# Output-projection blocks of the last layer as rows, and the final conversion to bf16 on ScalarE alone

## The chip, the cores and the metric

The kernel runs on one core of a Trainium2 chip. The metric is the device time of one execution in microseconds, the lower the better. The granted clock is the share of its full clock that TensorE had in a stretch by the profile.

## The reference

Four attention layers for one token, which use the weights and caches A, B, A, B in turn. Each layer normalizes x (640 values), makes 32 queries of 192, attends over a cache of 8192 keys and values per head, projects with wo and adds the result to x.

```python
def _A_ref(x, k_cache, v_cache, wq, wo):
    q = (x @ wq).reshape(B, Sq, Hq, Dh) ...                    # 640 -> 32 heads x 192
    scores = jnp.einsum("bhqd,bhkd->bhqk", q, k) * (Dh ** -0.5) # 8192 keys per head
    p = _softmax(scores, axis=-1)
    o = jnp.einsum("bhqk,bhkd->bhqd", p, v)
    return o.reshape(B, Sq, Hq * Dh) @ wo                       # 6144 -> 640

x = A_x
x = x + _A_ref(_layernorm(x, axis=-1), A_k_cache, A_v_cache, A_wq, A_wo)
x = x + _B_ref(_layernorm(x, axis=-1), B_k_cache, B_v_cache, B_wq, B_wo)
x = x + _A_ref(...)                                             # layer 2, A again
x = x + _B_ref(...)                                             # layer 3, B again
```

## The kernel before

The caches are streamed through eight slots of on-chip memory. VectorE multiplies k by the query, and TensorE sums the products through an identity matrix, makes the softmax's weighted sum of v, and projects. The projection is done in blocks of five pairs of heads (`wo` blocks 0, 1 and 2; the third is cut in two parts, the later one called `wob`) and a last pair (`wol`). PSUM is the memory into which the matmuls write; a bank is one piece of it, and a quadrant, in this text, is 32 neighbouring partitions (rows). The parts that matter:

```python
def op(self, fn, *events, ..., bank=()):
    for d in bank:                                  # one record per PSUM bank:
        self.wait(*[ev for q, ev in d.items() if q is not self])   # wait for every other engine's last use
    ...

def project(n, w, o, ev_o):                         # y as columns: 128 x 5 values
    PE.wait(ev_o, need(n), last["YB"])
    for i in range(k):                              # k = 15 in a whole block
        for c in range(DC):                         # DC = 5
            e = PE.op(... t.matmul(YB[:, c:c + 1], lhsT=t3[:, i, c:D:DC], rhs=o[:, i:i + 1], ...))
    freed[n] = e                                    # the slot of these weights is free
    return e

def project_row(n, w, o, ev_o):                     # y as two rows of 320, on partitions 0 and 32
    for i in range(k):
        for h in range(2):
            e = PE.op(... t.matmul(YR[32 * h:32 * h + 1, :], lhsT=o[:, i:i + 1],
                                   rhs=t3[:, i, h * HD:(h + 1) * HD], ...))
    return e

def to_row(ev):                                     # x + y so far, from columns to the rows
    e = DV.op(... z = x_true + YB[:, 0:DC], ev, ev_true, bank=YBu)
    ...                                             # z split into three bf16 parts on VectorE
    PE.op(... zero the rows ...)                    # 1 matmul
    for i in range(3):                              # 3 x 5 x 2 = 30 matmuls with the identity
        ...

elif n[0] == "wo":
    last["oT"] = (project_row if l == 3 and n[2] == 2 else project)(...)
    if l == 3 and n[2] == 1:
        to_row(last["oT"])
...                                                 # after the last layer:
a, m = slot[...][0:33, 0:HD], 192
return a, (DV.op(lambda v: v.tensor_copy(a[:, 0:m], YR[:, 0:m]), ev_y, last["oT"], bank=YBu),
           AC.op(lambda c: c.activation(a[:, m:], YR[:, m:], ACT.Copy), ev_y, last["oT"], bank=YBu))
```

Shortly before the end the kernel issues filler matmuls (`busy(16)` and `busy(6)`), whose result nobody reads.

## Time and profile before

| | before |
|---|---|
| time, 3 runs known at the prediction | 1985.24 us median, 1982.80 to 1987.34 |
| span of the profiled execution | 1980.6 us |
| bytes read, rate over the span | 848.36 MB, 428 GB/s |
| busiest compute engine | TensorE, 65% |
| last load lands | 1973.88 us |
| from there to the end of the span | 6.7 us |

### The profile page before, as it was taken

The page shows a single profiled execution, that of the slowest core. Times are in us where ns is not written, and L with a number is a line of the kernel's source. Part 1 is how long each engine was busy: PE and PEld are TensorE (multiplying, and loading weights), DVE is VectorE, ACT ScalarE, POOL GpSimd, SP SyncE. Part 2 cuts the span into 40 slices and gives each one's busy share as a digit, 9 for nine tenths or more (in the row PEclk, how much of TensorE's full clock was granted, in tenths as well). Part 3 has the DMA queues.
Part 4 walks back from the last instruction along what each step waited for, and adds up shares of the span by engine and source line. Part 5 has one row for each costly group of instructions (what it writes and reads, how often), then busy time and mean ns, then how long its engine had stood idle before and what let it go on. Part 6 is the DMA issues. An engine that isn't in the chain of part 4 may idle for free.

```text
span 1980.6 us, 13926 instructions
## 1 busy us (share of the span) xinstructions
PE 1282.8 (65%) x8335; PEld 148.6 (8%) x3249; DVE 1201.2 (61%) x1377; ACT 139.6 (7%) x462; POOL 4.5 (0%) x23
## 2 busy tenths in 40 slices
PE   3567476566466666666785675666676766667658
PEld 0001001000100100100020010010002001001001
DVE  3566466467166656566745565665764765665756
ACT  0000000000000000000010000000000100000000
POOL 0000000000000000000000000000000000000000
PEclk9787777778687777777887777877886877777778
DMA  9999999999999999999999999999999999999998
GB/s 413 437 432 430 430 430 432 436 430 428 435 431 431 430 435 433 428 433 433 427 408 432 427 430 431 430 430 431 431 431 428 436 429 434 432 432 431 431 434 364
DMA packets 26786, 849.25 MB, mean 429 GB/s; under 512 B 3042, under 2 KB 3044, under 8 KB 3812
## 3 DMA queue, kind: packets, MB, share of 16 engines
q1 hardware_dynamic: 26580, 848.38, 99.6%
q8 instruction: 45, 0.74, 0.2%
q14 instruction: 17, 0.14, 0.0%
q10 hardware_dynamic: 144, 0.00, 0.0%
HBM read 848.36 MB, written 0.00 MB: 428 GB/s over the span
## 4 chain that ended last, share of the span: by engine, by line
DMA 67%; PE 17%; DVE 15%; ACT 1%; issue 0%; SPq 0%
DMA pool<-in_B_k_cache_dram 27%; DMA pool<-in_A_v_cache_dram 22%; DMA pool<-in_A_k_cache_dram 13%; DVE pool L595 13%; PE S L58 7%; DMA pool<-in_B_v_cache_dram 6%; PE OY L58 5%; PE OY L674 3%; DVE acc L693 1%; ACT p_sb L632 1%; DVE s_sb L617 1%; PE OY L535 1%; PE S L608 0%; DVE m_bf L619 0%; PE QM L622 0%
## 5 line engine op out<-in xcount | busy, mean ns | idle before, releaser
L595 DVE TENSOR_TENSOR pool<-pool,q_sb 128x3072 bf16<-128x3072 bf16 x512 | 860.8, 1751 | 231.9 <-DMA pool<-in_B_k_cache_dram 133.3
L58 PE MATMUL S<-pool,ident 128*128 128x512 bf16 x2944 | 788.6, 425 | 20.4 <-DVE pool L595 18.8
L704 PE MATMUL TB<-acc,small 128*1 128x192 f32 x240 | 82.7, 495 | 212.0 <-DVE acc L693 212.0
L58 PE MATMUL OY<-pool,p_sb 128*16 128x512 bf16 x1920 | 198.8, 490 | 0.0
L608 PE MATMUL S<-pool,ident 128*128 128x512 bf16 x128 | 62.4, 488 | 207.7 <-DVE pool L595 207.6
L692 DVE TENSOR_SCALAR acc<-OY,small 128x192 f32<-128x192 f32 x64 | 26.7, 418 | 277.9 <-PE OY L58 248.0
L674 PE MATMUL OY<-pool,p_sb 128*16 128x512 bf16 (+1 forms) x1216 | 145.9, 488 | 64.3 <-DMA pool<-in_A_v_cache_dram 59.7
L693 DVE SCALAR_TENSOR_TENSOR acc<-OY,small,acc 128x192 f32<-128x192 f32 x424 | 177.0, 418 | 14.9
L617 DVE TENSOR_REDUCE s_sb<-S 128x64 f32<-128x512 f32 x128 | 87.8, 686 | 68.0 <-PE S L58 68.0
L524 ACT ACTIVATE q_sb<-QM 128x192 bf16<-128x192 f32 x60 | 19.8, 330 | 952.4 <-PE QM L518 952.4
L715 ACT ACTIVATE rows<-TB,small 1x192 bf16<-1x192 f32 x120 | 43.1, 405 | 587.7 <-PE TB L704 587.7
L688 DVE RECIPROCAL small<-TB 1x2 f32<-1x2 f32 x64 | 11.2, 175 | 94.7 <-PE TB L647 75.3
L632 ACT ACTIVATE p_sb<-s_sb,small 64x128 bf16<-64x128 f32 x128 | 55.7, 435 | 160.9 <-DVE small L626 160.1
L608 PEld LDWEIGHTS S<-pool,ident 128*128 128x128 bf16 x128 | 12.9, 101 | 682.9 <-DVE pool L595 619.9
L647 PE MATMUL TB<-small,ones 128*1 128x2 f32 x120 | 11.4, 165 | 74.1 <-ACT p_sb L632 74.1
L674 PEld LDWEIGHTS OY<-pool,p_sb 128*16 128x16 bf16 (+1 forms) x1216 | 38.9, 105 | 207.4 <-issue 133.1
L622 PE MATMUL QM<-ident,m_bf 128*64 128x64 bf16 x128 | 14.1, 217 | 54.4 <-DVE m_bf L619 53.8
L704 PEld LDWEIGHTS TB<-acc,small 128*1 128x1 f32 x240 | 19.8, 102 | 311.2 <-DVE acc L693 284.0
L535 PE MATMUL OY<-oT,pool 128*128 128x1 bf16 x825 | 34.9, 178 | 2.5 <-ACT oT L580 2.5
L626 DVE TENSOR_REDUCE small<-QM 128x1 f32<-128x64 f32 x64 | 14.3, 224 | 35.2 <-PE QM L622 35.2
L535 PEld LDWEIGHTS OY<-oT,pool 128*128 128x128 bf16 x825 | 33.9, 131 | 4.5 <-ACT oT L580 3.2
L518 PEld LDWEIGHTS QM<-rows,one_b 1*64 1x64 bf16 x120 | 6.2, 100 | 347.1 <-issue 341.2
(75 smaller groups left out, 205.0 us busy)
## 6 DMA issues: line engine op xcount, KB each, us to landing
pool<-in_B_k_cache_dram SPq DMA_DIRECT2D x28, 6144.0 KB, 38.1
pool<-in_B_v_cache_dram SPq DMA_DIRECT2D x28, 6144.0 KB, 33.5
pool<-in_A_v_cache_dram SPq DMA_DIRECT2D x27, 6144.0 KB, 27.6
pool<-in_A_k_cache_dram SPq DMA_DIRECT2D x34, 3072.0 KB, 19.9
pool<-in_A_k_cache_dram SPq DMA_DIRECT2D x14, 6144.0 KB, 36.5
pool<-in_A_v_cache_dram SPq DMA_DIRECT2D x10, 3072.0 KB, 14.3
pool<-in_B_k_cache_dram SPq DMA_DIRECT2D x8, 3072.0 KB, 22.4
pool<-in_A_wo_dram SPq DMA_DIRECT2D x6, 2400.0 KB, 22.1
```

The lines of the kernel that those rows point to most:

```text
L58: return t.add_instruction(mybir.InstMatmult(name=t.bass.get_next_instruction_name(), engine=mybir.EngineType.PE, ins=[t.lower_ap(rhs), t. ...
L524: lambda a: a.activation(q_sb[i][:], QM[:, 0:DH], ACT.Copy), e, last["q"][i], bank=QMu)
L535: e = PE.op(lambda t, i=i, c=c, f=y_first[0], fin=n[0] == "wol" and i == k - 1: t.matmul(YB[:, c:c + 1], lhsT=t3[:, i, c:D:DC], rhs=o[:, i ...
L595: e = DV.op(lambda v, d0=d0: v.tensor_tensor(k3[:, :, d0:d0 + QD], kin[:, :, d0:d0 + QD], q_sb[qi][:, d0:d0 + QD].unsqueeze(1).broadcast_t ...
L608: t.matmul(S[:, :], lhsT=ident[:], rhs=k3[:, :, d0:d0 + R], start=True, stop=fin) if d0 == 0 else
L617: lambda v, u=u: v.tensor_reduce(s[:, u * JU:(u + 1) * JU], SP_[u][:].rearrange("p (j r) -> p j r", r=R), AX.X, ALU.add), ev_S[p, u], last ...
L632: ev_p[p] = AC.op(lambda a, h=h, r=r: a.activation(p_sb[par][r, :, h], s[r, :], ACT.Exp, bias=negm[par][r, 0:1], accum_out=l_col[par][r, h ...
L674: t.matmul(o, lhsT=x, rhs=y, start=f, stop=fin) if c == 0 else
L692: v.tensor_scalar(acc[:], O[:, 0:DH], pick[:, 0:1], None, ALU.mult) if i == 0 else
L693: v.scalar_tensor_tensor(out=acc[:], in0=O[:, i * DH:(i + 1) * DH], scalar=pick[:, i:i + 1], in1=acc[:], op0=ALU.mult, op1=ALU.add)), e if ...
L704: e = PE.op(lambda t, h=h: t.matmul(TB[96:97, C_O + h * DH:C_O + (h + 1) * DH], lhsT=half[:, h:h + 1], rhs=acc[:], start=True, stop=True), ...
L715: last["TO"] = last["row_written"] = AC.op(lambda a, h=h: a.activation(orow[:, o0 + h * DH:o0 + (h + 1) * DH], TB[96:97, C_O + h * DH:C_O ...
```

## The change

The intent is to have one form of the projection in layer 3. Its blocks 0 and 1 become rows too, so that 30 matmuls replace 75 in each. The residual then no longer waits for block 1: it is turned into the row ahead of block 0, and VectorE's wait for the product falls away. The final conversion is one ScalarE copy in place of two half copies on two engines.

```diff
-            def to_row(ev):
-                e = DV.op(lambda v: v.tensor_tensor(z[:], x_true[:], YB[:, 0:DC], ALU.add), ev, ev_true, bank=YBu)
+            def to_row():
+                e = DV.op(lambda v: v.tensor_copy(z[:], x_true[:]), ev_true)
                 ...
-                PE.wait(e, ev_const)
+                PE.wait(e, ev_const, last["YB"])
@@ project_row
+                if n[0] == "wo" and n[2] < 2:
+                    freed[n] = e
@@ layer
-                    last["oT"] = (project_row if l == 3 and n[2] == 2 else project)(...)
-                    if l == 3 and n[2] == 1:
-                        to_row(last["oT"])
+                    if l == 3 and n[2] == 0:
+                        to_row()
+                    last["oT"] = (project_row if l == 3 else project)(...)
@@ end
-                a, m = slot[place[("wo", 3, 2)]][0:33, 0:HD], 192
-                return a, (DV.op(... tensor_copy(a[:, 0:m], YR[:, 0:m]) ...), AC.op(... a[:, m:], YR[:, m:] ...))
+                a = slot[place[("wo", 3, 2)]][0:33, 0:HD]
+                return a, AC.op(lambda c: c.activation(a, YR, ACT.Copy), ev_y, last["oT"], bank=YBu)
```

(The output transfer then waits for one event and not for two. Cuts are marked with dots.)

More of the change, by code (lines that the diff above doesn't have):

```diff
@@ L541, in project @@
                 return e
-            def to_row(ev):
-                src = z
-                e = DV.op(lambda v: v.tensor_tensor(z[:], x_true[:], YB[:, 0:DC], ALU.add), ev, ev_true, bank=YBu)
+            def to_row():
+                e = DV.op(lambda v: v.tensor_copy(z[:], x_true[:]), ev_true)
                 for i in range(3):
@@ L740, in layer @@
                     k = NW - NB[l] if n[2] == 2 else NW
-                    last["oT"] = (project_row if l == 3 and n[2] == 2 else project)(n, slot[place[n]][:, 0:k * D], oT[:, 0:k], last["oTw"])
-                    if l == 3 and n[2] == 1:
-                        to_row(last["oT"])
+                    if l == 3 and n[2] == 0:
+                        to_row()
+                    last["oT"] = (project_row if l == 3 else project)(n, slot[place[n]][:, 0:k * D], oT[:, 0:k], last["oTw"])
                 elif n[0] == "wob":
@@ L757, in layer @@
             if l + 1 == NL:
-                a, m = slot[place[("wo", 3, 2)]][0:33, 0:HD], 192
-                return a, (DV.op(lambda v: v.tensor_copy(a[:, 0:m], YR[:, 0:m]), ev_y, last["oT"], bank=YBu),
-                           AC.op(lambda c: c.activation(a[:, m:], YR[:, m:], ACT.Copy), ev_y, last["oT"], bank=YBu))
+                a = slot[place[("wo", 3, 2)]][0:33, 0:HD]
+                return a, AC.op(lambda c: c.activation(a, YR, ACT.Copy), ev_y, last["oT"], bank=YBu)
             ev_z = DV.op(lambda v: v.tensor_tensor(z[:], xc[:], YB[:, 0:DC], ALU.add), ev_y, ev_xc, bank=YBu)
@@ L767, in build @@
             ev_z, ev_true = layer(l, ev_z, ev_true)
-        e = SP.op(lambda s: s.dma_start(out[0, 0].rearrange("(h n) -> h n", h=2), ev_z[0:33:32, :]), *ev_true, sem=semOUT, inc=16)
+        e = SP.op(lambda s: s.dma_start(out[0, 0].rearrange("(h n) -> h n", h=2), ev_z[0:33:32, :]), ev_true, sem=semOUT, inc=16)
         SP.wait(e)
```

## The prediction

> **What bounds the kernel now.** I read the page from the top: the shares, the forty slices, then the chain of waits at its end, then the order of time around the places that the diff touches. The slices come first, because they say which resource never rests.
>
> ```profile
> PE 1282.8 (65%) x8335; PEld 148.6 (8%) x3249; DVE 1201.2 (61%) x1377; ACT 139.6 (7%) x462; POOL 4.5 (0%) x23
> DMA  9999999999999999999999999999999999999998
> HBM read 848.36 MB, written 0.00 MB: 428 GB/s over the span
> pool<-in_B_v_cache_dram SPq DMA_DIRECT2D x28, 6144.0 KB, 33.5
> ```
>
> No compute engine is busy for more than 65%, and the DMA row reads 9 in every slice but the last. 848.36 MB in 1980.6 us is 428 GB/s, so the span is the time of the transfers plus what lies before the first and after the last of them. The fourth line gives the depth of the queue: one load of 6144 KB (6.29 MB) takes 6.29/428 = 14.7 us at that rate, but the median from issue to landing is 33.5 us. So a load is issued with more than one other load ahead of it, and a delay of its issue by a few us leaves the stream unbroken. Only two kinds of change move the time: fewer bytes or a gap in that stream, and work after the last load has landed. The diff changes no byte, and a comparison of the instruction orders shows the DMA-issuing engine's own list of instructions the same in both kernels.
>
> The work after the last landing is read from the chain of waits, in order of time:
>
> ```profile
> 1936.56 37.33 DMA pool<-in_B_v_cache_dram
> ...
> 1975.73 0.89 PE TB L700 x12
> 1976.62 1.20 PE OY L568 x16
> 1977.82 0.02 issue
> 1977.84 0.36 DVE pool L759
> 1978.20 0.02 issue
> 1978.22 0.27 ACT pool L760
> ```
>
> The last load lands at 1973.88. From there to the end of the span are 6.7 us, all serial. The reader should see the last three pieces of work: the 16 row matmuls of layer 3's last block, then VectorE's copy of 192 columns to bf16, and then ScalarE's copy of the other 128. They are written as two halves of one job on two engines, but they run one after the other. The waits say so too: ScalarE sat idle "1.30 <-DVE pool L759" before its copy, though the matmuls had been over for 0.4 us by then. The cause is in the code: each operation on the row's PSUM bank first waits for the last operation of every other engine on that bank, reads included. The split therefore gains nothing.
>
> The third view is the order of time around layer 3's second wo block, where the diff has its largest piece:
>
> ```profile
> 1802.01 3.16 PE L535 MATMUL OY<-oT,pool 128*128 128x1 bf16 x75 [0.28 <-ACT oT L580]
> 1805.20 0.33 SPq L376 DMA_DIRECT2D pool<-in_B_v_cache_dram  x1
> 1805.20 0.16 DVE L546 TENSOR_TENSOR small<-small,OY 128x5 f32<-128x5 f32 x1 [6.84 <-PE OY L535]
> ...
> 1806.44 0.45 PE L552 MATMUL OY<-ident,zero 128*33 128x320 bf16 x1 [1.27 <-DVE part L548]
> 1806.82 1.48 PEld L557 LDWEIGHTS OY<-ident,part 128*1 128x1 bf16 x30 [0.28 <-issue]
> 1806.82 1.76 PE L557 MATMUL OY<-ident,part 128*1 128x64 bf16 x30
> 1809.15 13.44 DVE L595 TENSOR_TENSOR pool<-pool,q_sb 128x3072 bf16<-128x3072 bf16 x8 [2.77 <-DMA pool<-in_B_k_cache_dram]
> ```
>
> 75 column matmuls (3.16 us) end the block and release its weights' slot, so the next v load is issued. Then VectorE adds and splits the residual (six operations, until 1806.38) and TensorE turns it into a row (until 1808.58). After that VectorE still waits 2.77 us, and for a DMA: the next k tile lands at 1809.15, whatever this block does.
>
> **What the Trainium skill says.** "DMA: Bandwidth & Descriptors", section Bandwidth, measures 425 GB/s for 16 MB with one core streaming, and puts the ceiling at 435. The trace agrees: 428 over the whole span and 430 to 437 in most slices. There is no room left in the stream.
>
> "PSUM — Partial Sum Buffer", section on PSUM bank collisions, says that two engines must not touch the same bank and quadrant at once, two readers included. Both copies read the same bank in the same two quadrants, so the wait between them is needed and not an oversight; the trace shows it kept.
>
> "ScalarE: Activation LUTs", section What ACT_TABLE_LOAD costs, gives 186 ns + 0.833 ns per column for an ACTIVATE with immediate scale and bias. The trace is a little below: 185 ns for 15 columns (198 by the formula), 270 for 128 (293) and 330 for 192 (346). For 320 columns the formula gives 453 ns; less the 16 to 23 ns by which it is high at 192 and 128 columns, I take 0.43 us.
>
> "TensorE: Matmul & The Clock Gate", Part 1, says that the clock falls to half after an idle stretch of about 3.4 us. The stretches agree: the granted clock is 0.50 through both wo blocks, at 1651.8 to 1655.1 and at 1802.0 to 1805.2, and 1.00 in the tail, where the kernel runs filler matmuls first. This matters for the price of a row matmul.
>
> **The change part by part.**
>
> Part one, blocks 0 and 1 as rows. Each loses 75 column matmuls at 3.16/75 = 42 ns and gains 30 row matmuls of 320 columns. In the tail 16 of those took 1.20 us with 0.30 us for a single one, so (1.20 - 0.30)/15 = 60 ns from one to the next, at clock 1.00. At 0.50 I take twice that, 120 ns: 29 x 0.12 + 0.45 = 3.9 us (estimate). So a block becomes about 0.8 us longer, not shorter, if the clock stays down; with a full clock it would be 29 x 0.06 + 0.30 = 2.0 us, 1.1 us shorter. The instruction count alone, 30 for 75, misleads here.
>
> Part two, the residual moved. At block 0 its six VectorE operations (1805.20 to 1806.38, so 1.2 us; the first becomes a copy of as many elements) need no product of the block and can run as soon as VectorE has finished the fifth pair's accumulation, at 1648.2. VectorE then idles 9.85 us until a k tile lands at 1658.06, so they are hidden. TensorE's 31 matmuls (0.38 us to the next start and 1.76 us, some 2.1 us) now stand between the columns and the block's own products. The block's end, and with it the issue of the v load that waits for its slot, moves from 1655.06 to about 1655.1 + 2.1 - 0.2 (the wait for oT, now covered) + 0.8 = 1657.8, 2.7 us later. The queue then still holds the k load that was issued at 1644.62 and lands only at 1687.1. So nothing empties. TensorE's next matmuls begin at 1659.88, which is 2 us after.
>
> At block 1 the v load is issued some 0.8 us later than at 1805.20 (or 1.1 us earlier, at a full clock), and TensorE is free at about 1806 in place of 1808.6. VectorE's 6.84 us wait there is gone. Its next product still starts when the k tile lands at 1809.15, so this is worth 0 us.
>
> Part three, the final row. On the path, from 1977.84 to 1978.49, are 0.36 + 0.02 + 0.27 = 0.65 us. One ScalarE copy of 320 columns replaces it with 0.43 us and the same start: after a PE result the two engines begin within 0.02 us of each other in the trace (1976.62 to 1976.65 for ScalarE, 1977.82 to 1977.84 for VectorE). Saved: 0.22 us. The output transfer waits for one semaphore in place of two, which I count as 0.
>
> Sum: 0 + 0 - 0.22 = -0.2 us, or 0.01%. From the median of 1985.24 that gives 1985.0.
>
> **The rivals.** First, the later v load at block 0 opens a gap in the stream. For it speaks only that the issue does move, by an estimated 2.7 us. Against it stands the backlog: the loads issued at 1637.67 and 1644.62 are both still unfinished at 1655.06, near 2 x 14.7 = 29 us of work. Even if all of it came through, the time would be 1987.7, still within 2%.
>
> Second, the freed time counts in full: the removed VectorE wait (6.84 us), the shorter TensorE work after block 1 (2.6 us) and the tail (0.2 us) would give 1975.6, 0.5% faster. For it speaks that VectorE is busy 61% and holds 15% of the chain. Against it: the wait after it is for a DMA (the 2.77 us at 1809.15), and time freed on an engine that waits for data returns as a longer wait. I think it unlikely.
>
> Third, ScalarE could be slower from PSUM over 33 partitions than I reckon. If its copy took 0.65 us, the tail would be as before: 1985.2.
>
> **Range and chances.** All that the change can do is smaller than the noise: the three runs before lie at 1982.80, 1985.24 and 1987.34, 4.5 us apart. The range follows from that spread and not from the rivals: 1985.0 with 4.5 us to each side, 1980.5 to 1989.5. A change of 2% would be 40 us. Neither rival comes near it, so within 2% gets 0.99, and each side 0.005.
>
> **What would show it right or wrong.** The tail: ScalarE's copy of 33x320 starts some 0.03 us after the last row matmul and lasts 0.41 to 0.46 us, with no VectorE operation near it; from the last landing to the span's end pass 6.5 us in place of 6.7. The blocks: 30 row matmuls in 3.4 to 4.2 us at a granted clock of 0.50; if they take about 2 us, my scaling with the clock fails. At block 0 TensorE's 31 residual matmuls come ahead, and the v load is issued 2 to 3 us later after the wait for the matmuls' end; its landing does not move against its neighbours. At block 1 VectorE waits once, for the k tile. The rate stays at 428 GB/s over the span. I am wrong if the DMA row shows a slice under 9 around 1640 to 1700, if the chain passes through the row matmuls of blocks 0 or 1, or if the time moves by more than the runs scatter.

## The result, and the profile after

| | before | after |
|---|---|---|
| time, 6 runs each | 1983.33 us median, 1982.80 to 1987.34 | 1983.21 us median, 1982.22 to 1984.94 |
| ratio | | 0.9996, 95% interval 0.9983 to 1.0009 |
| span of the profiled execution | 1980.6 us | 1980.6 us |
| last load lands | 1973.88 | 1974.19 |
| last landing to end of span | 6.7 us | 6.4 us |

A ratio is the mean time of one kernel's runs over that of the other's of the same rounds, so it is not quite the ratio of the medians quoted. Executions over 1.5% slower than the fastest of the same kernel are left out of the means.

The time is the same within what the timer can tell. The changed kernel is right. Its stream of transfers, from the page's forty slices (first the busy tenths of the DMA engines, then the bytes they moved):

```profile
DMA  9999999999999999999999999999999999999998
GB/s 413 435 435 429 430 430 433 436 428 429 436 430 431 430 435 433 427 433 432 426 412 431 426 429 432 431 428 432 431 430 428 435 431 435 431 432 432 431 432 367
HBM read 848.36 MB, written 0.00 MB: 428 GB/s over the span
```

Nothing has changed there. Blocks 0 and 1 of layer 3 fall into slices 34 and 37 of 40, and no slice from there on dips but the last, as before. Next the order of time around block 0 (start, length, engine, line, operation; in brackets the idle time before it and what ended it), first before, then after:

```profile
1644.62 0.33 SPq L376 DMA_DIRECT2D pool<-in_B_k_cache_dram  x1
...
1651.88 3.16 PE L535 MATMUL OY<-oT,pool 128*128 128x1 bf16 x75 [0.28 <-ACT oT L580]
1655.06 0.33 SPq L376 DMA_DIRECT2D pool<-in_B_v_cache_dram  x1
1658.06 3.43 DVE L595 TENSOR_TENSOR pool<-pool,q_sb 128x3072 bf16<-128x3072 bf16 x2 [9.85 <-DMA pool<-in_B_k_cache_dram]
```

```profile
1645.01 0.33 SPq L376 DMA_DIRECT2D pool<-in_B_k_cache_dram  x1
...
1648.52 0.16 DVE L545 COPY small<-small 128x5 f32<-128x5 f32 x1
...
1651.92 0.45 PE L551 MATMUL OY<-ident,zero 128*33 128x320 bf16 x1
1652.30 1.76 PE L556 MATMUL OY<-ident,part 128*1 128x64 bf16 x30
1653.81 4.07 PE L567 MATMUL OY<-pool,oT 128*1 128x320 bf16 x30
1657.92 0.33 SPq L376 DMA_DIRECT2D pool<-in_B_v_cache_dram  x1
1658.28 5.09 DVE L596 TENSOR_TENSOR pool<-pool,q_sb 128x3072 bf16<-128x3072 bf16 x3 [8.58 <-DMA pool<-in_B_k_cache_dram]
```

The residual's VectorE work (from 1648.52) is done while VectorE would wait for the k tile. TensorE's part of it and the rows follow each other, and the v load goes out when the rows end. Counted from the k load ahead of it, it is issued 12.9 us later; before it was 1655.06 - 1644.62 = 10.4 us. Block 1 after, in the same view:

```profile
1802.26 4.16 PE L567 MATMUL OY<-pool,oT 128*1 128x320 bf16 x30 [0.28 <-ACT oT L581]
1806.46 0.33 SPq L376 DMA_DIRECT2D pool<-in_B_v_cache_dram  x1
1810.01 3.43 DVE L596 TENSOR_TENSOR pool<-pool,q_sb 128x3072 bf16<-128x3072 bf16 x2 [11.41 <-DMA pool<-in_B_k_cache_dram]
```

VectorE's wait of 6.84 us for the block's products is gone. In its place stands one wait of 11.41 us for the k tile: the freed time has come back as a longer wait for data. (The tile lands 0.86 us later than before. Already the k load of block 0, which no part of the change precedes, was issued 0.39 us later in this trace, and the last landing is later by 0.31 us.) The waits of the DMA-issuing engine tell the same of the v loads behind both blocks (who waited for whom: us in total, times, longest), first before, then after:

```profile
SPq L376 <- PE OY L535: 20.2, 2, 10.1
```

```profile
SPq L376 <- PE OY L567: 23.7, 2, 12.6
```

The queue's issuer waited 3.5 us longer in all for the two blocks, and the stream did not notice. Last, the end of the chain of waits after the change:

```profile
1936.94 37.25 DMA pool<-in_B_v_cache_dram
...
1976.93 1.20 PE OY L567 x16
1978.13 0.02 issue
1978.15 0.43 ACT pool L760
```

One copy of 0.43 us stands where VectorE's 0.36, a gap of 0.02 and ScalarE's 0.27 stood. Around blocks 0 and 1 the chain runs along the k loads (one of 42.31 us from 1645.01 on) and not through the row matmuls, as the prediction had it.

### The profile page after: what moved, and what is told of

Its sections match the earlier page's. It is cut to its first block, busy times and chain, and to the rows that moved or that the text cites. A ratio compares the mean times of both kernels' runs of the same rounds, so it can differ in the third digit from the quotient of the medians.

```text
span 1980.6 us, 13743 instructions
## 1 busy us (share of the span) xinstructions
PE 1288.7 (65%) x8245; PEld 146.4 (7%) x3159; DVE 1201.3 (61%) x1376; ACT 139.9 (7%) x462; POOL 4.5 (0%) x23
## 3 DMA queue, kind: packets, MB, share of 16 engines
HBM read 848.36 MB, written 0.00 MB: 428 GB/s over the span
## 4 chain that ended last, share of the span: by engine, by line
DMA 67%; PE 19%; DVE 12%; ACT 1%; issue 0%; SPq 0%
DMA pool<-in_B_k_cache_dram 27%; DMA pool<-in_A_v_cache_dram 22%; DMA pool<-in_A_k_cache_dram 13%; DVE pool L596 10%; PE S L58 10%; DMA pool<-in_B_v_cache_dram 6%; PE OY L58 5%; PE OY L675 3%; DVE acc L694 1%; ACT p_sb L633 1%; DVE s_sb L618 1%; PE S L609 1%; PE OY L535 0%; DVE m_bf L620 0%; PE QM L623 0%
## 5 line engine op out<-in xcount | busy, mean ns | idle before, releaser
L693 DVE TENSOR_SCALAR acc<-OY,small 128x192 f32<-128x192 f32 x64 | 26.7, 418 | 281.1 <-PE OY L58 251.6
L689 DVE RECIPROCAL small<-TB 1x2 f32<-1x2 f32 x64 | 11.2, 175 | 94.9 <-PE TB L648 75.2
L609 PEld LDWEIGHTS S<-pool,ident 128*128 128x128 bf16 x128 | 12.9, 101 | 683.1 <-DVE pool L596 589.1
L535 PE MATMUL OY<-oT,pool 128*128 128x1 bf16 x675 | 28.6, 178 | 1.9 <-ACT oT L581 1.9
L535 PEld LDWEIGHTS OY<-oT,pool 128*128 128x128 bf16 x675 | 27.8, 131 | 3.8 <-ACT oT L581 2.5
```

Of the source, the lines that this page charges most:

```text
L535: e = PE.op(lambda t, i=i, c=c, f=y_first[0], fin=n[0] == "wol" and i == k - 1: t.matmul(YB[:, c:c + 1], lhsT=t3[:, i, c:D:DC], rhs=o[:, i ...
L609: t.matmul(S[:, :], lhsT=ident[:], rhs=k3[:, :, d0:d0 + R], start=True, stop=fin) if d0 == 0 else
L693: v.tensor_scalar(acc[:], O[:, 0:DH], pick[:, 0:1], None, ALU.mult) if i == 0 else
```

## The experiments

My theory: the stream of loads sets the time, a backlog of nearly 30 us in its queue hides whatever the wo blocks do, and the only part of the change on the path is the final copy, some 0.2 us. The rivals: a later issue of a load counts in full; TensorE's work does not matter at all; the rows themselves gain time that the later issue eats up.

**How late may a load be issued?** Two kernels take the changed kernel and make block 0 later, by filler matmuls of which the result is not read.

```diff
                     if l == 3 and n[2] == 0:
+                        busy(88)      # late40: busy(180)
                         to_row()
```

> The changed kernel with 88 filler matmuls (about 20 us of TensorE: some 8 at half clock, the rest at full) ahead of the residual's turn to a row at layer 3's first wo block, so that the v load that waits for the slot of this block's weights is issued some 18 us later. Backlog theory: the k load ahead of it in the queue lands only near 1687, so the stream does not empty; ratio to before 0.999 to 1.001, no gap in the transfers. Rival (a later issue counts in full): +18 us, ratio 1.009. By the way: the 30 row matmuls then run at a granted clock of 1.00 and take 2.0 to 2.2 us in place of 4.07.

Measured: right output, 1982.41 us median against 1983.21 for the kernel before, ratio 0.9998 (0.9983 to 1.0013). From the order of time:

```profile
1651.99 20.19 PE L58 MATMUL S<-ident 128*128 128x512 bf16 x87
...
1673.16 2.23 PE L567 MATMUL OY<-pool,oT 128*1 128x320 bf16 x30
1675.43 0.33 SPq L376 DMA_DIRECT2D pool<-in_B_v_cache_dram  x1
```

The load is issued 17.5 us later than in the changed kernel (1657.92), and the last one still lands at 1974.14, against 1974.19. So 17.5 us cost nothing that shows. The rows also took 2.23 us at the full clock that the fillers brought, against 4.07 us at half clock. That is just above the 2.0 to 2.2 expected. The column matmuls gain nothing from the clock: 75 of them took 3.16 us at half clock, 42 ns each, and in layer 1 of the kernel before 50 took 2.16 us at a granted clock of 1.00, 43 ns each. So the rows are the shorter form at full clock and the longer one at half clock.

> The same with 180 fillers (about 40 us). Now the v load is issued near 1695, after the last queued load has landed near 1687. Backlog theory: the first 30 us are hidden and the rest comes through, +8 to +14 us (ratio 1.004 to 1.007), and the transfers show one gap of about that length. Rival that a later issue counts in full: +38 us, ratio 1.019. Rival that nothing on TensorE matters for the time at all: 1.000.

Measured: right output, 1994.69 us, ratio 1.0058 (1.0043 to 1.0073), which is 11.5 us. The issue and the stretches around the gap (stretch, length, then busy time and count of each engine; the last three numbers are granted clock, DMA share and GB/s):

```profile
1695.82 0.33 SPq L376 DMA_DIRECT2D pool<-in_B_v_cache_dram  x1
```

```profile
1660.00:1680.00 20.00, 20.00 (x94) 0.00 (x0) 12.09 (x8) 0.00 (x0) 0.00 (x0) 1.00 1.01 433
1680.00:1690.00 10.00, 10.00 (x48) 0.00 (x0) 0.00 (x0) 0.00 (x0) 0.00 (x0) 1.00 0.35 152
1690.00:1700.00 10.00, 10.00 (x93) 2.26 (x62) 0.00 (x0) 0.00 (x0) 0.00 (x0) 1.00 0.44 159
1700.00:1710.00 10.00, 7.74 (x55) 0.55 (x15) 2.07 (x5) 1.31 (x5) 0.00 (x0) 1.00 0.91 393
```

The load goes out 37.9 us later than in the changed kernel. The last load lands at 1985.43, so 11.2 us later. The backlog hid 37.9 - 11.2 = 26.7 us and not one more: the gap is in the stream, where the DMA share falls to 0.35 and 0.44 (from 1686 to 1694 nothing moves at all). Both rivals fall here: a late issue counts neither in full (it would be 38 us) nor never. The third rival falls with `late20`: a later issue within the backlog eats nothing up, so a gain by the rows clear of the timer's noise would have shown.

**Does the tail count in full?** The changed kernel with its last copy made 21 times.

```diff
                 e = AC.op(lambda c: c.activation(a, YR, ACT.Copy), ev_y, last["oT"], bank=YBu)
+                for i in range(20):
+                    e = AC.op(lambda c: c.activation(a, YR, ACT.Copy), e, bank=YBu)
```

> The changed kernel with the final ScalarE copy made 21 times in a row, each waiting for the one before: 20 x about 0.46 us = 9.2 us more after the last landing. If work after the last landing counts in full: +8.5 to +10 us, ratio 1.0043 to 1.005, while 20 us of TensorE work at the wo block cost nothing. If the tail were hidden too: 1.000.

Measured: right output, 1993.04 us, ratio 1.0051 (1.0036 to 1.0066), which is 10.1 us.

```profile
1980.30 1.00 PE L567 MATMUL OY<-rows,oTl 128*1 128x320 bf16 x6
1981.35 0.43 ACT L760 ACTIVATE pool<-OY 33x320 bf16<-33x320 f32 x1 [1.97 <-PE OY L567]
1981.81 9.20 ACT L762 ACTIVATE pool<-OY 33x320 bf16<-33x320 f32 x20
```

The 20 copies added 9.20 us to the chain, and the timer saw them. It is slightly above my 8.5 to 10, but its interval (7.1 to 13.1 us) holds that range. So 9 us at the end cost about 9 us within what the timer can tell, and 17.5 us at the wo block showed no cost. The trace also shows something I had not expected. The last row matmuls were slower here (6 in 1.00 us; before and after, 6 in 0.57). The last part of this section comes back to it.

**The two parts alone.** `rows_only` is the changed kernel with the split copy; `copy_only` is the kernel before with ScalarE's single copy.

```diff
# rows_only, against the changed kernel
-  return a, AC.op(... c.activation(a, YR, ACT.Copy) ...)
+  return a, (DV.op(... a[:, 0:192], YR[:, 0:192] ...), AC.op(... a[:, 192:], YR[:, 192:] ...))
# copy_only, against the kernel before
-  return a, (DV.op(... a[:, 0:192], YR[:, 0:192] ...), AC.op(... a[:, 192:], YR[:, 192:] ...))
+  return a, AC.op(... c.activation(a, YR, ACT.Copy) ...)
```

> The changed kernel with the final copy split between VectorE and ScalarE as before; the blocks and the residual as changed. Ratio to before 0.999 to 1.001. From the last landing to the span's end 6.7 us as before, ScalarE's copy starting 0.03 us after VectorE's ends. The two blocks' row matmuls take 4.0 to 4.2 us at a granted clock of 0.50.

> The kernel before with ScalarE alone making the final copy; blocks and residual as before. Ratio 0.999 to 1.001. From the last landing to the span's end 6.4 to 6.5 us: all of the change's gain on the path is here, 0.2 to 0.3 us. If the rows of blocks 0 and 1 helped the time, this kernel would be slower than the changed one by more than that; I expect no difference that shows.

Measured: ratios 1.0004 (0.9990 to 1.0017) and 1.0002 (0.9987 to 1.0017), both right. The chain's end, first of `rows_only`:

```profile
1973.99 0.04 issue
...
1976.77 2.25 PE OY L567 x9
1979.01 0.02 issue
1979.04 0.36 DVE pool L760
1979.40 0.02 issue
1979.42 0.27 ACT pool L761
```

and of `copy_only`:

```profile
1974.69 0.04 issue
...
1977.43 1.20 PE OY L568 x16
1978.63 0.02 issue
1978.65 0.43 ACT pool L759
```

The copies are as expected: 0.65 us in two steps against 0.43 us in one. For `copy_only` the last landing to the end of the span takes 1981.1 - 1974.69 = 6.4 us, the same as in the changed kernel, so the whole gain on the path comes from the copy. For `rows_only` I had expected 6.7 us and it took 1981.8 - 1973.99 = 7.8 us. The 1.05 us more lie in the row matmuls of the tail, 2.25 us in place of 1.20, and not in the copy. The rows of its blocks 0 and 1 took 4.10 and 4.16 us (granted clock 0.53 and 0.50), as expected, and the time is no shorter than before.

**Can both engines convert at once?** The wait between the two halves comes from the record kept per bank. Here VectorE takes the row on partition 32 and ScalarE the row on partition 0, which lie in two quadrants of the bank, with no wait for each other.

```diff
-  return a, AC.op(lambda c: c.activation(a, YR, ACT.Copy), ev_y, last["oT"], bank=YBu)
+  return a, (DV.op(lambda v: v.tensor_copy(a[32:33, :], YR[32:33, :]), ev_y, last["oT"], bank=PE_only),
+             AC.op(lambda c: c.activation(a[0:1, :], YR[0:1, :], ACT.Copy), ev_y, last["oT"], bank=PE_too))
```

(`PE_only` and `PE_too` are copies of the bank's record with TensorE's last use alone.)

> The final copy on both engines again, but VectorE takes the row at partition 32 and ScalarE the row at partition 0 (all 320 columns each), so that they share no quadrant of the bank and need no wait for each other. They should start within 0.05 us of each other; ScalarE 0.43 us, VectorE about [...]0.48 us (from the 192 columns in 0.35 us[...]). Tail from the last landing to the span's end as in the changed kernel, 6.4 to 6.5 us: two engines at once buy nothing, as the time goes by columns. The output stays right. If the bank and not the quadrant were what collides, the output would be wrong.

Measured: right output, ratio 1.0003 (0.9986 to 1.0019).

```profile
1978.89 0.43 ACT L763 ACTIVATE pool<-OY 1x320 bf16<-1x320 f32 x1 [0.92 <-PE OY L567]
1978.89 0.48 DVE L762 CAST pool<-OY 1x320 bf16<-1x320 f32 x1 [2.17 <-PE OY L567]
```

They start together, as expected, and gain nothing: one partition takes ScalarE 0.43 us for 320 columns, and so do 33. The last landing to the end is 1981.4 - 1974.93 = 6.5 us. This agrees with "PSUM — Partial Sum Buffer", section on PSUM bank collisions, by which two engines may access different quadrants of one bank at once. What two readers of the same quadrant would do without the wait, no run here tried.

**Why is the tail sometimes 1 us longer?** In three of the eight traces up to here (`late40`, `tail10`, `rows_only`) the last 16 row matmuls took 2.25 us. The other five took 1.20 us, and all have the same tail up to there. The granted clock tells the two cases apart; first the kernel before, then `rows_only` (the columns are those of the stretches above):

```profile
1975.00:1976.60 1.60, 0.87 (x14) 0.86 (x16) 0.64 (x2) 0.00 (x0) 0.00 (x0) 1.00 0.20 80
1976.60:1977.80 1.20, 1.20 (x17) 0.56 (x16) 0.00 (x0) 0.27 (x1) 0.00 (x0) 1.00 0.00 0
```

```profile
1975.00:1976.60 1.60, 0.77 (x12) 0.77 (x12) 0.74 (x2) 0.00 (x0) 0.00 (x0) 0.94 0.26 107
1976.60:1977.80 1.20, 1.20 (x12) 0.63 (x13) 0.00 (x0) 0.27 (x1) 0.00 (x0) 0.50 0.00 0
```

The clock fell from 1.00 to 0.50 in the middle of the tail. I tried more fillers (`fill` changes two places at once), and none before the last landing:

```diff
 # fill, three times (fill_a, fill_b, fill_c)
-                            busy(6)
+                            busy(8)
                         PE.wait(need(("vq", l)))
@@ after the last products
+                if l == 3 and p == NPAIR - 1:
+                    busy(3)
 # nofill
-                        if l == 3:
-                            busy(6)
```

> In three of the eight traces so far the 16 last row matmuls took 2.25 us instead of 1.20, with a granted clock of 0.50. Here the changed kernel has 8 filler matmuls in place of 6 before the last load lands, and 3 more after its products, while VectorE accumulates. If short idle stretches of TensorE in the tail let the clock fall, it stays at 1.00: 1.20 us in every trace, last landing to end 6.4 us. Rival: the clock falls by its own timing and fillers of this length do not hold it; some of the traces show 2.25 us. Median at best 0.4 us below the changed kernel (3/8 of 1.05 us), which timing cannot show: ratio 0.999 to 1.001.

> The same kernel again, for another trace of the tail: row matmuls 1.20 us if fillers hold the clock, 2.25 us in some if they don't.

> The same kernel a third time: 1.20 us if fillers hold the clock.

> The changed kernel without the 6 filler matmuls before the last load lands. If the fillers keep the clock up, TensorE is idle from 1972 to 1974 and the last row matmuls run at half clock: 2.25 us, and from the last landing to the end about 7.5 us. Rival (clock has its own timing): 1.20 us in about five of eight traces. Ratio to before 1.000 to 1.001.

Measured, all right: `fill_a` ratio 0.9997 (0.9983 to 1.0011), `fill_b` and `fill_c` one look each at 1983.51 and 1983.19 us, `nofill` ratio 1.0001 (0.9988 to 1.0015). The row matmuls in the chain, of `fill_a`, `fill_b`, `fill_c` and `nofill`:

```profile
1976.93 1.20 PE OY L567 x16
```

```profile
1978.04 1.20 PE OY L567 x16
```

```profile
1977.73 1.20 PE OY L567 x16
```

```profile
1978.20 2.25 PE OY L567 x9
```

All four came out as the fillers would have it, and from the last landing to the end of the span pass 6.4 us in all three of `fill` and 7.7 us in `nofill`. But if the clock had fallen by its own timing in three of eight executions, three good ones in a row would still come in 0.24 of such trials (5/8 cubed), and one slow one in 3/8. That fillers hold the clock is therefore likely and not settled. In the median nothing clear of noise shows (`nofill` lies 0.9 us above `fill_a`, whose own runs lie 1.9 us apart), and I don't claim that `fill` beats either kernel.

The traces hold one more hint, looked for only afterwards: how long TensorE sat idle between its last filler and the last landing. Here is `quadrants`, which kept the clock, and then `rows_only`, which lost it:

```profile
1974.97 0.82 PE L675 MATMUL OY<-pool,p_sb 128*4 128x384 bf16 x16 [1.00 <-DMA pool<-in_B_v_cache_dram]
```

```profile
1974.03 0.82 PE L675 MATMUL OY<-pool,p_sb 128*4 128x384 bf16 x16 [0.93 <-DMA pool<-in_B_v_cache_dram]
```

The other four traces that kept the clock show 0.54 to 0.80 us there, the other two that lost it (`tail10` and `late40`) 1.04 and 1.06 us; the three of `fill` show 0.27 to 0.51 us and `nofill`, counted from its last matmul, 2.35 us. A longer idle stretch goes with a lost clock, but the two lines above stand in the wrong order, so its length alone does not decide.

## Why the prediction was right

- **The bound.** Right. The stream carries the same 848.36 MB at 428 GB/s; the profiled spans are 1980.6 us both. `late20`, `late40` and `tail10` show that delay on TensorE enters the time only where it empties the queue or comes after the last landing.
- **The rows of blocks 0 and 1.** Estimated 3.9 us each at half clock; measured 4.07 and 4.16 us (granted clock 0.54 and 0.50), so longer than the 3.16 us of the 75 columns, though there are fewer. At full clock 2.0 us estimated, 2.23 us in `late20`. The sign rested on the clock and not on the count.
- **The later v loads.** Against the k load ahead, block 0's moved by 12.9 - 10.4 = 2.5 us (predicted 2.7), and block 1's by (1806.46 - 1795.00) - (1805.20 - 1794.77) = 1.0 us (predicted 0.8).
- **The backlog.** I reckoned near 29 us from two loads of 14.7 us; `late40` gives 26.7 us beyond the changed kernel's own issue, which already is 2.5 us late. That agrees.
- **The freed VectorE wait is worth 0.** Right: it came back as an 11.41 us wait for the k tile.
- **The final copy.** Predicted 0.43 us and a gain of 0.22 us; measured 0.43 and, from landing to end, 6.7 to 6.4 us. The gain is nearer 0.3 us (1980.6 - 1973.88 = 6.72 against 6.41), since the output's transfer also starts sooner after the copy's end, 0.03 us in place of 0.08 (0.07 in `rows_only`, 0.03 in `copy_only`). I had counted the dropped second wait as 0. It also makes one exception to my sentence that the DMA-issuing engine's list is the same in both kernels.
- **The number.** 1985.0 predicted, 1983.21 measured. The predicted step was -0.2 us and is in the trace. The 1.8 us between come from the base: the three runs that I had lay higher (1985.24) than the six known now (1983.33). The timer itself can't confirm a step of 0.2 us; its interval is some 2.6 us to either side. What the timer shows is only that nothing large came in.
- **What I missed.** I took the full clock in the tail as given, because one trace showed it. It is lost in some executions, and that costs 1.05 us, about four times what the change gains there. What I drew from the skill on the clock, an idle stretch of about 3.4 us, does not explain this loss (see the last section).

## What to carry to other kernels

Before pricing the work that a change moves, find out how much backlog the queue of loads holds where it lands: here some 27 us of delay were free, and the next microsecond was not. Two engines that read one bank under one record of waits are one engine with a handover. And price a matmul at the clock granted in that stretch: 30 row matmuls of 320 columns took 4.1 us at half clock and 2.2 us at full, while the column matmuls that they replace took 42 to 43 ns each at either.

## What the Trainium skill lacked or had wrong

- "TensorE: Matmul & The Clock Gate", Part 1, has the clock fall after at least one idle window of about 3.4 us. In `rows_only` it fell with no idle stretch of TensorE longer than 1 us (0.93 and 0.98 us in the trace). Further down, in its section "A second HAM failure mode: psum-queue depth-cycling" (HAM is its word for the part that sets this clock), the page has short idle stretches between groups of matmuls make the clock go up and down, but nowhere does it say how much work within a window keeps it up. In the 3.5 us after the last filler TensorE was busy for 1.6 us in `rows_only`, where the clock fell, for 1.5 us in `quadrants` and for 2.0 us before, where it did not. So the busy share alone is not the rule either; the rule is open.
- "DMA: Bandwidth & Descriptors", section Bandwidth, says in one sentence that for loads from HBM the HBM side, about 358 GB/s, binds. On one core 848.36 MB moved at 428 GB/s, which fits the same section's single-core figure of 425 GB/s. The section's own note under its table gives about 358 GB/s to each of two cores that stream at once, so the sentence lacks that condition. Single slices of the profiles here reach 436 and 437 GB/s, slightly above the skill's ceiling of 435.
- "ScalarE: Activation LUTs", section What ACT_TABLE_LOAD costs: 186 ns + 0.833 ns per column is 453 ns for 320 columns; the copies took 0.43 us, for 1 partition as for 33. The formula is about 20 ns high here, as it is at 128 and 192 columns.
